# The last row block's sums and stores by two batches, stores from two queues in turn

## Chip, cores and metric

The kernel runs on one core of one Trainium2 chip. The metric is the device time of one execution in microseconds. Each kernel was executed several times; medians are given. Where one execution was profiled, times inside it are counted from the start of its span. The profile page prints a span to 0.1 us; where tails are compared below, they are taken from the unrounded trace.

## The reference

```python
B, S, D = 8, 4224, 192              # batches, tokens, channels
x  = causal 7-tap convolution of x along the tokens, taps = softmax(weight) per head
theta = x @ w_theta                 # 192 x 192
zr, zi = x * cos(theta), x * sin(theta)
y  = w_tok_r @ zr + w_tok_i @ zi    # per batch, 4224 x 4224 token mixing
u  = x + y
out = u + max(u @ w_ch, 0)          # 192 x 192
```

The token mixing is nearly all of the work.

## The kernel before

The 33 row blocks of 128 tokens are finished one after another. For a finished block, `u` (128 x 1536, fp32) lies in the SBUF tile `pv`. It is cast to fp16 (`ub`), transposed (`uT`), multiplied by `wch` into PSUM (`v`), and then, for each half `g` of the eight batches, summed and stored:

```python
def channel_mix(tT, w):
    v = banks("v")                       # one PSUM tile of two banks, two such tiles in turn
    for k in range(2):                   # k: two batches each
        for b in range(2):
            for i in range(2):
                pe(nc.tensor.matmul(v[:, k, b * D : (b + 1) * D], lhsT=tT[:, 3 * k + b + i, :],
                                    rhs=w[:, 2 * b + i, :], start=(i == 0), stop=(i == 1)))
    return v[:, :, 0 : 2 * D]
...
def output(self, i, g):                  # g: four batches, 128 x 768
    u = self.pv[i][:, g * GC : (g + 1) * GC]
    ub = u.rearrange("p (k n) -> p k n", k=2)
    dve(nc.vector.scalar_tensor_tensor(
        out=ub, in0=channel_mix(self.uT[i][:, 6 * g : 6 * g + 6, :], wch), scalar=0.0, in1=ub,
        op0=ALU.max, op1=ALU.add))
    rows = slice(self.tbs[i] * P, (self.tbs[i] + 1) * P)
    nc.sync.dma_start(out=out[g * GB : (g + 1) * GB, rows, :].rearrange("b s d -> s b d"),
                      in_=u.rearrange("p (b d) -> p b d", d=D))
```

`dve` and `pe` keep the order in which the program emits the instructions of an engine. The products of the token mixing (line 443 in the profile) go to other PSUM tiles, named `y`, and their results are added to `pv` by line 408.

Of the kernel before, what the change touches and what calls it, by code (L numbers as in the profile page):

```python
# [10 lines left out]
ALU = mybir.AluOpType  # L11
# [5 lines left out]
def kernel(  # L17
# [23 lines left out]
    nc = tc.nc  # L41
    B, S, D = x.shape
# [13 lines left out]
    GB = 4  # L56
    NG = B // GB
    GC = GB * D
# [8 lines left out]
    NSTEP = start[-1] + NU  # L67
# [10 lines left out]
    def in_order(engine, ins):  # L78
        if engine in last:
            tc.add_manual_dep(ins.ins, last[engine].ins.name, NOSYNC, reason="order")  # L80
        last[engine] = ins
        return ins

    def pe(ins):
        return in_order("pe", ins)

    def dve(ins):
        return in_order("dve", ins)
# [23 lines left out]
    def banks(name, dtype=F32):  # L112
        return mmpool.tile([P, 2, PC if dtype == F32 else 2 * PC], dtype,
                           name=name, tag="mm")
# [9 lines left out]
    wch = constp.tile([P, 4, D], F16, name="wch")  # L124
# [10 lines left out]
    def channel_mix(tT, w):  # L135

        v = banks("v")
        for k in range(2):
            for b in range(2):
                for i in range(2):  # L140
                    pe(nc.tensor.matmul(  # L141
                        v[:, k, b * D : (b + 1) * D], lhsT=tT[:, 3 * k + b + i, :],
                        rhs=w[:, 2 * b + i, :], start=(i == 0), stop=(i == 1),
                    ))
        return v[:, :, 0 : 2 * D]
# [139 lines left out]
    class Step:  # L285
# [185 lines left out]
            crossed(self.uT[i], self.ub[i])  # L471

        def output(self, i, g):
            u = self.pv[i][:, g * GC : (g + 1) * GC]
            ub = u.rearrange("p (k n) -> p k n", k=2)
            dve(nc.vector.scalar_tensor_tensor(  # L476
                out=ub, in0=channel_mix(self.uT[i][:, 6 * g : 6 * g + 6, :], wch), scalar=0.0, in1=ub,
                op0=ALU.max, op1=ALU.add,
            ))
            rows = slice(self.tbs[i] * P, (self.tbs[i] + 1) * P)  # L480
            nc.sync.dma_start(
                out=out[g * GB : (g + 1) * GB, rows, :].rearrange("b s d -> s b d"),
                in_=u.rearrange("p (b d) -> p b d", d=D),
            )

        def outputs(self):

# [75 lines left out]
    for a in range(2):  # L563
        nc.gpsimd.affine_select(
            out=sel, in_=sel, pattern=[[1, Q - 1 + 2 * WR]], channel_multiplier=-1,
# [4 lines left out]
    for a, lo in ((0, True), (1, False)):  # L570
        nc.gpsimd.affine_select(
            out=block[:, a : a + 1], in_=block[:, a : a + 1], pattern=[[0, 1]],
# [7 lines left out]
    def idle(n):  # L580
# [7 lines left out]
        out=wmax, in_=wsb, axis=mybir.AxisListType.X, op=ALU.max  # L588
    ))
    dve(nc.vector.tensor_tensor(  # L590
        out=wsb, in0=wsb, in1=wmax[:, :].unsqueeze(2).to_broadcast([P, H, KS]),
# [6 lines left out]
        out=wsum, in_=wsb, axis=mybir.AxisListType.X, op=ALU.add  # L598
# [5 lines left out]
        out=wdiag, in0=wsb[0:KS, :, :],  # L604
        in1=ident[0:KS, 0:KS].unsqueeze(1).to_broadcast([KS, H, KS]), op=ALU.mult,
# [3 lines left out]
        out=wcol, in_=wdiag, axis=mybir.AxisListType.X, op=ALU.add  # L609
# [5 lines left out]
    for q in range(Q):  # L615
# [7 lines left out]
        out=bands[:, :, 0, :], in0=bv, scalar1=block[:, 0:1]  # L623
    ))
    act(nc.scalar.activation(  # L625
        out=bands[:, :, 1, :], in_=bv, func=AT.Copy, scale=block[:, 1:2]
# [109 lines left out]
```

## Time and profile before

| | |
|---|---|
| three executions, us | 1447.4, 1448.13, 1449.99 (median 1448.13) |
| span of the profiled one | 1446.43 us |
| TensorE busy | 98% of the span |
| end of the last matmul | 1440.85 us |
| from there to the end of the span ("the tail" below) | 5.58 us |

The lines behind this are in the prediction. When a change touches only the end of a program, read the timeline of the end and not the shares of the whole.

### The profile page before, as it was taken

How to read it: one execution, taken by the hardware profiler on the slowest of the kernel's cores; microseconds unless marked ns; L12 is line 12 of the kernel's file. 1: busy time of each engine (PE TensorE's matmuls, PEld its weight loads, DVE VectorE, ACT ScalarE, POOL GpSimd, SP SyncE). 2: the span in 40 equal slices, each digit the busy share in tenths (PEclk: the TensorE clock that was granted, in tenths of full speed). 3: DMA queues.
4: the chain of work that ended last, by engine and by line, in shares of the span. 5: the costliest groups of instructions: out<-in, count | busy, mean ns of one | idle time of the engine just before them, and what ended most of it. 6: DMA issues, size and time to landing. Idle time of an engine off the chain costs nothing.

```text
span 1446.4 us, 23748 instructions
## 1 busy us (share of the span) xinstructions
PE 1416.3 (98%) x9809; PEld 887.9 (61%) x9809; DVE 979.2 (68%) x1051; ACT 315.5 (22%) x379; POOL 435.1 (30%) x655
## 2 busy tenths in 40 slices
PE   7899999999999999999999999999999999999997
PEld 5556666666666666666666666666666666666665
DVE  6893555545548777866666657877777667767686
ACT  5861101111134254000000004435210110010133
POOL 7431211111233232432433342233323123213120
PEclk9999999999999999999999999999999999999999
DMA  9986756465699998998899989999999999998893
GB/s 173 227 178 145 146 103 149 90 149 97 137 231 219 214 250 217 228 254 183 213 256 213 242 143 245 228 188 234 279 216 206 209 204 221 204 203 194 166 222 125
DMA packets 272029, 281.99 MB, mean 195 GB/s; under 512 B 106672, under 2 KB 240176, under 8 KB 271920
## 3 DMA queue, kind: packets, MB, share of 16 engines
q0 software_dynamic: 162464, 92.15, 48.4%
q1 hardware_dynamic: 71824, 178.88, 35.1%
q10 hardware_dynamic: 37632, 9.44, 4.1%
q8 instruction: 77, 1.26, 0.3%
q14 instruction: 32, 0.26, 0.1%
HBM read 245.49 MB, written 108.13 MB: 244 GB/s over the span
## 4 chain that ended last, share of the span: by engine, by line
PE 89%; DVE 4%; DMA 3%; POOL 2%; ACT 1%; issue 1%; SPq 0%; DVEq 0%; ACTq 0%; POOLq 0%
PE y L443 82%; PE v L141 5%; PE pc L210 1%; PE tp L165 1%; POOL st L323 1%; DMA xw<-in_x_dram 1%; DVE z L257 1%; DVE wt L336 1%; DVE pv L408 1%; ACT z L246 1%; DVE z L251 0%; DVE pv L476 0%; DVE wt L348 0%; POOL xw L197 0%; DMA xs<-z 0%
## 5 line engine op out<-in xcount | busy, mean ns | idle before, releaser
L443 PE MATMUL y<-z,wt 128*128 128x384 f16 x7656 | 1283.6, 326 | 10.6 <-DVE pv L408 7.5
L443 PEld LDWEIGHTS <-wt 128*128 128x128 f16 x7656 | 740.8, 98 | 488.6 <-issue 10.6
L408 DVE TENSOR_TENSOR pv<-y,pv 128x768 f32<-128x768 f32 x324 | 308.9, 954 | 323.6 <-PE y L443 282.8
L336 DVE STREAM_TRANSPOSE wt<-st 128x1408 f16<-128x1408 f16 (+7 forms) x224 | 327.8, 1465 | 48.5 <-PE y L443 39.0
L323 POOL DMA_DIRECT2D st<-in_moe_w_tok_r_dram x232 | 132.5, 578 | 466.1 <-DVE wt L336 461.0
L323 POOL DMA_DIRECT2D st<-in_moe_w_tok_i_dram x232 | 132.7, 578 | 404.4 <-DVE wt L336 388.9
L348 DVE TENSOR_TENSOR wt<-wt 128x1408 f16<-128x1408 f16 (+7 forms) x216 | 176.7, 818 | 40.8 <-PE y L443 38.4
L151 ACT ACTIVATE z<-pc 128x768 f16<-128x768 f32 x65 | 53.2, 819 | 387.2 <-PE pc L210 386.9
L151 ACT ACTIVATE ub<-pv 128x768 f16<-128x768 f32 x63 | 50.2, 835 | 333.0 <-DVE pv L408 310.4
L406 ACT ACTIVATE pv<-y 128x768 f32<-128x768 f32 x66 | 54.0, 819 | 282.0 <-PE y L443 282.0
L141 PEld LDWEIGHTS <-uT 128*128 128x128 f16 x1056 | 91.0, 98 | 25.8 <-issue 7.9
L386 POOL TENSOR_TENSOR pv<-pv,xr 128x1536 f32<-128x1536 f32 x24 | 74.5, 3105 | 68.6 <-DVE pv L476 22.1
L197 POOL DMA_DIRECT2D xw<-in_x_dram x132 | 76.4, 585 | 31.0 <-DMA xw<-xw 8.7
L476 DVE SCALAR_TENSOR_TENSOR pv<-v,pv 128x768 f32<-128x768 f32 x66 | 62.9, 954 | 27.5 <-PE v L141 27.1
L257 DVE TENSOR_TENSOR z<-z 128x768 f16<-128x768 f16 x132 | 73.4, 556 | 3.6
L151 ACT ACTIVATE uT<-tp 128x1536 f16<-128x1536 f16 (+1 forms) x48 | 58.2, 1215 | 74.4 <-PE tp L165 74.4
L246 ACT ACTIVATE z<-v,half_pi 128x768 f16<-128x768 f32 x66 | 59.8, 907 | 41.2 <-PE v L141 40.8
L251 DVE TENSOR_TENSOR z<-z 128x1536 f16<-128x1536 f16 x66 | 60.0, 947 | 7.5 <-ACT z L246 7.5
L141 PE MATMUL v<-wth,uT 128*128 128x192 f16 x528 | 55.0, 248 | 4.4 <-ACT z L246 3.0
L141 PE MATMUL v<-wch,uT 128*128 128x192 f16 x528 | 54.2, 246 | 2.1 <-DVE pv L476 1.2
L246 ACT ACTIVATE z<-v 128x768 f16<-128x768 f32 x66 | 53.4, 809 | 0.0
L210 PE MATMUL pc<-xw,bands 96*64 96x192 f16 x528 | 35.8, 258 | 2.6 <-ACT bands L625 1.1
(44 smaller groups left out, 142.4 us busy)
## 6 DMA issues: line engine op xcount, KB each, us to landing
part<-pv SPq DMA_DIRECT2D x79, 768.0 KB, 4.3
pv<-part SPq DMA_DIRECT2D x79, 768.0 KB, 6.1
out_dram<-pv SPq DMA_DIRECT2D x66, 384.0 KB, 4.3
st<-in_moe_w_tok_r_dram POOLq DMA_DIRECT2D x136, 176.0 KB, 5.5
st<-in_moe_w_tok_i_dram POOLq DMA_DIRECT2D x136, 176.0 KB, 5.1
xs<-z SPq DMA_DIRECT2D x132, 96.0 KB, 4.5
xw<-in_x_dram POOLq DMA_DIRECT2D x121, 96.0 KB, 6.1
xr<-xs SPq DMA_DIRECT2D x24, 384.0 KB, 3.7
```

The lines of the kernel that those rows point to most:

```text
L141: pe(nc.tensor.matmul(v[:, k, b * D : (b + 1) * D], lhsT=tT[:, 3 * k + b + i, :], rhs=w[:, 2 * b + i, :], start=(i == 0), stop=(i == 1),))
L151: act(nc.scalar.activation(out=out, in_=in_, func=AT.Copy))
L197: nc.gpsimd.dma_start(out=self.xw[lo : lo + n, h, :, :], in_=x[:, t0 : t0 + n, :].rearrange("b s d -> s b d"),)
L246: act(nc.scalar.activation(**args))
L257: dve(nc.vector.tensor_tensor(out=z[:, o, :], in0=z[:, a, :], in1=z[:, b, :], op=ALU.subtract))
L323: pool(nc.gpsimd.dma_start(out=st[a * Q : (a + 1) * Q, 0:nb, :, 0:n] .rearrange("i r bt s -> i (r bt) s"), in_=w[self.tbs[0] * P : (self.t ...
L336: dve(nc.vector.transpose(self.w[name][:, 0 : self.n, :, :], self.st[int(name[1])][:, int(name[0]) - 1, :, 0 : self.n * Q] .rearrange("p b ...
L348: dve(nc.vector.tensor_tensor(out=self.w[name][:, 0 : self.n, :, :], in0=self.w[a][:, 0 : self.n, :, :], in1=self.w[b][:, 0 : self.n, :, : ...
L386: ins = pool(nc.gpsimd.tensor_tensor(out=self.pv[i], in0=self.pv[i], in1=self.xr[i], op=ALU.add))
L408: dve(nc.vector.tensor_tensor(out=o, in0=yv, in1=o, op=ALU.add))
L443: pe(nc.tensor.matmul(y[cn][:, q, 0:BH], lhsT=self.w[wn][:, c, :, :].rearrange("p bt i -> p (bt i)"), rhs=chunks[k].z[:, zn, q * BH : (q + ...
L476: dve(nc.vector.scalar_tensor_tensor(out=ub, in0=channel_mix(self.uT[i][:, 6 * g : 6 * g + 6, :], wch), scalar=0.0, in1=ub, op0=ALU.max, o ...
```

## The change

The intent: let the last stores start earlier and be shorter. For the last row block only, each sum of four batches becomes two sums of two batches, and each is stored as soon as it is done, by ScalarE's queue and SyncE's in turn.

```diff
-            u = self.pv[i][:, g * GC : (g + 1) * GC]
-            ub = u.rearrange("p (k n) -> p k n", k=2)
-            dve(nc.vector.scalar_tensor_tensor(
-                out=ub, in0=channel_mix(self.uT[i][:, 6 * g : 6 * g + 6, :], wch), scalar=0.0, in1=ub,
-                op0=ALU.max, op1=ALU.add,
-            ))
+            u = self.pv[i][:, g * GC : (g + 1) * GC].rearrange("p (k n) -> p k n", k=2)
+            v = channel_mix(self.uT[i][:, 6 * g : 6 * g + 6, :], wch)
             rows = slice(self.tbs[i] * P, (self.tbs[i] + 1) * P)
-            nc.sync.dma_start(
-                out=out[g * GB : (g + 1) * GB, rows, :].rearrange("b s d -> s b d"),
-                in_=u.rearrange("p (b d) -> p b d", d=D),
-            )
+            ends = self.t == NSTEP - 1
+            for k in (slice(0, 1), slice(1, 2)) if ends else (slice(0, 2),):
+                dve(nc.vector.scalar_tensor_tensor(
+                    out=u[:, k, :], in0=v[:, k, :], scalar=0.0, in1=u[:, k, :],
+                    op0=ALU.max, op1=ALU.add,
+                ))
+                b = slice(g * GB + 2 * k.start, g * GB + 2 * k.stop)
+                dma = nc.scalar.dma_start if ends and k.start == 0 else nc.sync.dma_start
+                dma(
+                    out=out[b, rows, :].rearrange("b s d -> s b d"),
+                    in_=u[:, k, :].rearrange("p k (b d) -> p (k b) d", d=D),
+                )
```

## The prediction

> **What bounds the kernel now.** I read first the summary page: what the whole span is made of, and the size of the groups that the change touches.
>
> ```profile
> span 1446.4 us, 23748 instructions
> PE 1416.3 (98%) x9809; PEld 887.9 (61%) x9809; DVE 979.2 (68%) x1051; ACT 315.5 (22%) x379; POOL 435.1 (30%) x655
> ...
> PE 89%; DVE 4%; DMA 3%; POOL 2%; ACT 1%; issue 1%; SPq 0%; DVEq 0%; ACTq 0%; POOLq 0%
> ...
> L476 DVE SCALAR_TENSOR_TENSOR pv<-v,pv 128x768 f32<-128x768 f32 x66 | 62.9, 954 | 27.5 <-PE v L141 27.1
> ...
> out_dram<-pv SPq DMA_DIRECT2D x66, 384.0 KB, 4.3
> ```
>
> TensorE is busy for 98% of the span and makes 89% of the chain that ended last: this is a matmul-bound kernel. The change touches two of the 66 sums of line 476 and two of the 66 stores, both of the last row block, and no matmul. So only the tail, after the last matmul, can move. Second, the timeline of the last microseconds (start, length, engine, line, operation, count, idle before):
>
> ```profile
> 1438.32 0.96 DVE L476 SCALAR_TENSOR_TENSOR pv<-v,pv 128x768 f32<-128x768 f32 x1 [0.98 <-PE v L141]
> ...
> 1439.33 1.52 PE L141 MATMUL v<-wch,uT 128*128 128x192 f16 x16 [0.21 <-DVE pv L476]
> ...
> 1440.19 1.82 DVE L476 SCALAR_TENSOR_TENSOR pv<-v,pv 128x768 f32<-128x768 f32 x2 [0.91 <-PE v L141]
> ```
>
> TensorE ends at 1439.33 + 1.52 = 1440.85. The first of the two last sums starts at 1440.19, the second follows with no wait, and both are done at 1442.01. The second needs matmuls that were done before it started, so VectorE itself sets this stretch. Third, the store's line, asked for the last two stores alone (issue length in ns, issue start, then microseconds from issue to landing), and, in a second fence, the waits of the SyncE queue (total us, times, longest):
>
> ```profile
> L481 SPq DMA_DIRECT2D out_dram<-pv x1: 372/372/372, 1441.2 to 1441.2; - x1
> ...
> DMA to landing us min/median/max: 2.5/2.5/2.5
> ...
> L481 SPq DMA_DIRECT2D out_dram<-pv x1: 372/372/372, 1442.0 to 1442.0; - x1
> ...
> DMA to landing us min/median/max: 2.7/2.7/2.7
> ```
>
> ```profile
> SPq L731 <- DMA out_dram<-pv: 2.2, 1, 2.2
> ```
>
> After the last store is issued, the program only waits for it: 2.2 us on SyncE, then the closing steps. The store lands at 1442.0 + 2.7 = 1444.7, and the span ends at 1446.4, so 1.7 us of closing follow. Fourth, busy shares by stretch; in each line the last two numbers are the DMA share and GB/s, and the one before them TensorE's granted clock:
>
> ```profile
> 1441.40:1441.50 0.10, 0.00 (x0) 0.00 (x0) 0.10 (x1) 0.00 (x0) 0.00 (x0) 1.00 0.01 0
> ...
> 1442.00:1442.10 0.10, 0.00 (x0) 0.00 (x0) 0.01 (x1) 0.00 (x0) 0.00 (x0) 1.00 0.09 31
> 1442.10:1442.20 0.10, 0.00 (x0) 0.00 (x0) 0.00 (x0) 0.00 (x0) 0.00 (x0) 1.00 0.73 253
> ...
> 1443.10:1443.20 0.10, 0.00 (x0) 0.00 (x0) 0.00 (x0) 0.00 (x0) 0.00 (x0) 1.00 1.09 354
> ...
> 1444.20:1444.30 0.10, 0.00 (x0) 0.00 (x0) 0.00 (x0) 0.00 (x0) 0.00 (x0) 1.00 0.47 139
> ```
>
> The DMA engines are empty from 1441.4 to 1442.1, then full without a gap to about 1444.3. Both last stores run back to back through them: 2 x 393,216 bytes in 2.2 us, about 360 GB/s. This is the real limit of the tail. The last store does not wait for its own issue; it waits behind the one before it (2.7 us to landing where the undisturbed one has 2.5). Hence the end is: first data of the second-last store, plus 2.2 us of transfer, plus 0.4 us to landing (1444.3 to 1444.7), plus 1.7 us of closing. Only the start of that busy stretch is open to the change.
>
> **What the Trainium skill says.** "DMA: Bandwidth & Descriptors", section "Issuing engines are not separate DMA queues", says that transfers started from several engines share the same 16 DMA engines, and that a second issuing engine saves only the issue time. The trace agrees as far as it goes: two adjacent stores run at one store's rate (369 and 376 GB/s in neighbouring stretches), but both came from one queue. "Perfetto Trace Analysis", section "DMA Optimizations", says that splitting a DMA may let a part start sooner where the DMA engines are idle. That is the idle stretch from 1441.4 to 1442.1 here. The same page, section "DMA Instruction — HWDGE (DVE, Sync)", shows a descriptor generator shared by the issuing sequencers, with a lock wait inside the profiled issue time. This trace has 372 ns for most stores, but 712 ns for the one issued at 1437.4, 1.0 us after another, which might be such a wait. "VectorE: DVE Perf Modes", section "Why PSUM operands drop a tier", allows fp32 with a PSUM operand one element per cycle; at that page's 0.96 GHz, 768 columns take 800 ns. The measured 954 ns leaves about 154 ns fixed. Back to back the second sum started before the first had ended: 1.82 - 0.96 = 0.86 us from start to start, so only about 0.06 us of the fixed part shows.
>
> **The change part by part.** I compared the instruction order of both kernels, apart from line numbers. TensorE and GpSimd are the same, instruction by instruction. VectorE has four sums of 128x384 in place of two of 128x768; the second and fourth have no wait of their own. SyncE keeps two stores, halved, and ScalarE gets two at its end, where it is idle (the timeline has its last work at 1439.15 for 0.81 us). Nothing earlier changes. Each first half waits for all eight matmuls of its result, since its partner has no wait of its own; so no sum starts earlier than 1440.19.
>
> - Sums: half a sum is estimated as 400 + 154 = 554 ns, and 400 + 60 = 460 ns from start to start. Starts 1440.19, 1440.65, 1441.11, 1441.57; ends about 1440.74, 1441.20, 1441.66, 1442.12. Two more instructions cost 2 x 0.06 = 0.12 us at the end, but the first part is ready at 1440.74, not at 1441.15: 0.41 us earlier.
> - Issues: 0.03 to 0.05 us after each end, at about 1440.78, 1441.24, 1441.70 and 1442.16. In before, first data came 0.9 us after the issue started (1441.2 to 1442.1). I take this for all four, from either queue.
> - Transfers: first data could come at 1441.68, 1442.14, 1442.60 and 1443.06. The store ahead of them has left the engines by 1441.4, so the first starts at once. Each needs 2.2/4 = 0.55 us, more than the 0.46 us between them, so the engines are full from 1441.68 until 1441.68 + 2.2 = 1443.88. The last quarter could start at 1443.06 and finish at 1443.61 by itself, so the queue of bytes, and not the later last sum, still sets the end.
> - Sum: 1444.3 - 1443.9 = 0.4 us earlier; landing and closing move along. The 0.12 us on VectorE stay beside the transfers and cost nothing.
>
> The total is 1448.13 - 0.4 = 1447.7 us, 0.03% less.
>
> **The rivals.**
> First: the halves are worth more. If the end were set by the last store alone, without a queue ahead of it, halving it would save 0.55 us and the later sum would return 0.12: also 0.43 us. It would show as empty DMA stretches between the quarters. The gapless stretch speaks against it, and the time would hardly tell.
> Second: issue costs take the gain back. Four issues 0.46 us apart share a generator; if each took 0.7 us, as the one store of 712 ns did, issues from 1440.78 on would run to about 1443.6, first data of the last would come 0.55 us after that (the gap from an issue's end to its data in before: 1441.57 to 1442.1), and its end at 1444.7: 0.4 us slower, 1448.5. For it speaks the one 712; against it, the pair 0.86 us apart with 372 each.
> Third: nothing is visible. A ScalarE issue may have a longer way to first data, and its two halves may land late through one slow engine (two stores of the tail took 3.1 us, not 2.5). Then the gain is 0 to 0.2 us, 1448.0.
> None of them reaches 2%, which is 29 us: from the last sum's start to the end of the span there are only 6 us.
>
> **Range and chances.** The effect is between -0.5 and +0.4 us. Three runs of before span 1447.4 to 1449.99, so the spread of runs is larger than the effect. I take 1446.3 to 1449.3. A 2% change would need something that the instruction order excludes, or a slow execution: faster 0.003, same 0.992, slower 0.005.
>
> **What would show the steps right or wrong.** In the changed kernel's profile: four sums of 128x384 of about 554 ns, the last ending near 1442.1 of a comparable span; DMA busy from about 1441.7, gapless for 2.2 us; the last landing 0.4 us earlier measured from the last matmul's end (3.85 us after it in before, about 3.45 then). Wrong would be: issues much over 372 ns, a gap between the quarters, ScalarE's data more than 0.9 us after its issue, or a sum longer than 600 ns. The total itself can fail by the spread of runs alone.

## The result, and the profile after

| | before | changed |
|---|---|---|
| executions, us | 1447.4, 1448.13, 1449.57, 1449.99 | 1447.82, 1449.12, 1450.23, 1452.22 |
| median | 1448.85 | 1449.67 |
| span of the profiled one | 1446.43 | 1446.11 |
| tail | 5.58 | 5.29 |

The ratio is 1.0007 with a 95% interval from 0.9989 to 1.0026: no difference is seen. (A ratio is the mean time of one kernel's fast executions over that of the other's in the same rounds, so not quite the ratio of the medians.) "Within 2%" is as foreseen, but the median of 1449.67 lies above the stated range, which ended at 1449.3. And yet the profiled execution is shorter than that of before, and its tail is too.

The timeline of the changed kernel's end (columns as in the prediction):

```profile
1439.30 1.52 PE L141 MATMUL v<-wch,uT 128*128 128x192 f16 x16 [0.22 <-DVE pv L480]
...
1440.16 1.95 DVE L480 SCALAR_TENSOR_TENSOR pv<-v,pv 128x384 f32<-128x384 f32 x4 [0.91 <-PE v L141]
1440.75 1.31 ACTq L486 DMA_DIRECT2D out_dram<-pv  x2
```

The last matmul ends at 1439.30 + 1.52 = 1440.82, against 1440.85 before: nothing ahead of the tail has moved in this pair of profiles. The four half sums run from 1440.16 to 1442.11 (estimated: 1442.12), and the first half store is issued at 1440.75 (estimated: 1440.78), where the first store of before was issued at 1441.2.

The first and the last of the four stores (issue time, start, and time to landing), then the shares by stretch at the two ends of their transfer (the last two numbers are the DMA share and GB/s):

```profile
L486 ACTq DMA_DIRECT2D out_dram<-pv x1: 397/397/397, 1440.8 to 1440.8; - x1
DMA to landing us min/median/max: 2.0/2.0/2.0
...
L486 SPq DMA_DIRECT2D out_dram<-pv x1: 372/372/372, 1442.1 to 1442.1; - x1
DMA to landing us min/median/max: 2.4/2.4/2.4
```

```profile
1441.60:1441.70 0.10, 0.00 (x0) 0.00 (x0) 0.10 (x2) 0.00 (x0) 0.00 (x0) 1.00 0.13 46
1441.70:1441.80 0.10, 0.00 (x0) 0.00 (x0) 0.10 (x1) 0.00 (x0) 0.00 (x0) 1.00 0.89 307
...
1443.80:1443.90 0.10, 0.00 (x0) 0.00 (x0) 0.00 (x0) 0.00 (x0) 0.00 (x0) 1.00 0.94 259
1443.90:1444.00 0.10, 0.00 (x0) 0.00 (x0) 0.00 (x0) 0.00 (x0) 0.00 (x0) 1.00 0.04 8
```

The engines fill at 1441.7 and empty at 1443.9. The estimate was 1441.68 to 1443.88. Measured from the last matmul's end, the last data are through after 3.14 us, where it was 3.50 before: 0.36 us earlier. The last store lands after 3.69 us, where it was 3.85: only 0.16 us earlier, because its landing came 0.55 us after the last data and not 0.34. What follows the landing then took 1.60 us and not 1.73, so 0.29 us reach the end of the span (5.58 - 5.29). Up to the last data the mechanism is the predicted one, and the change gains about 0.3 us. The landing did not move along as predicted. The question is why the total is outside the range.

One more line of this profile will be needed below. In the view of the DMA queues from 1442.0 to 1444.4, an instruction fetch (kind "instruction") lies among the last stores; it started 3.05 us after the last matmul's end. In the kernel before there is none in that stretch.

```profile
q14 instruction: 1, 0.01, 1.4%
```

### The profile page after: what moved, and what is told of

Its sections match the earlier page's. It is cut to its first block, busy times and chain, and to the rows that moved or that the text cites. A ratio compares the mean times of both kernels' runs of the same rounds, so it can differ in the third digit from the quotient of the medians.

```text
span 1446.1 us, 23755 instructions
## 1 busy us (share of the span) xinstructions
PE 1415.9 (98%) x9809; PEld 887.7 (61%) x9809; DVE 979.4 (68%) x1053; ACT 315.4 (22%) x379; POOL 434.9 (30%) x655
## 4 chain that ended last, share of the span: by engine, by line
PE 89%; DVE 3%; DMA 3%; ACT 2%; POOL 1%; issue 1%; SPq 0%; DVEq 0%; ACTq 0%; POOLq 0%
PE y L443 82%; PE v L141 5%; PE pc L210 1%; PE tp L165 1%; DMA xw<-in_x_dram 1%; DMA xw<-xw 1%; POOL st L323 1%; ACT z L246 1%; DVE pv L408 1%; DVE z L257 1%; DVE z L251 1%; DMA pv<-part 1%; DVE wt L336 1%; DVE pv L480 0%; DMA st<-in_moe_w_tok_r_dram 0%
## 5 line engine op out<-in xcount | busy, mean ns | idle before, releaser
L480 DVE SCALAR_TENSOR_TENSOR pv<-v,pv 128x768 f32<-128x768 f32 (+1 forms) x68 | 63.1, 931 | 27.5 <-PE v L141 27.0
```

## The experiments

Every kernel below gave correct results. Runs r1 to r8 were on one chip, r9 to r11 on a second, r12 and r13 on a third; ratios are always against the kernel before on the same chip. Profiles of r5, r6 and r9 to r11 come from single executions, of which I use only the traces, not the times. The theory to test: the change moves only the tail, and the miss is scatter between executions. The rival: the change costs about 1 us somewhere ahead of the tail.

### r1: the changed kernel again

No edit.

> The changed kernel, run again with more rounds, to tell an effect from spread. Measure 1: the tail, from the end of the last matmul to the end of the span in the profile; it was 5.58 us before (1446.43 - 1440.85) and 5.29 us after (1446.11 - 1440.82). Measure 2: the ratio of the times to those of the kernel before. Theory (the change moves only the tail, by -0.3 us, and the miss of the range is spread between executions): tail 5.2 to 5.4 us, start of the last matmuls of the kernel unchanged within the spread, ratio 0.999 to 1.001 with an interval that holds 1. Rival (the change costs about 1 us somewhere ahead of the tail, which would explain 1449.67): ratio 1.0005 or more again, with the interval above 1, and the last matmul ending 1 us later than before in the profile.

Measured: median 1449.23 us (1448.13 to 1450.48), ratio 0.9999 (0.9986 to 1.0013), tail 5.28 us. The last matmul ended 0.43 us later than in the profile of before, and all of that had arisen in the first 48 us, long before any changed instruction. The rival's extra microsecond is not there.

### r2: the kernel before against itself

No edit to the kernel before.

> The kernel before against itself: a control without any change. Theory of spread: the ratio is off 1 by up to 0.001 either way, single runs lie from about 1447.4 to 1452 us, and the tail is 5.5 to 5.7 us. Rival (executions of one program agree to a few tenths of a us, and the 1.5 us between the two medians were the change): all runs within 1 us, ratio within 0.0002 of 1.

Measured: median 1450.39 us, single executions from 1448.14 to 1457.82 us, ratio 1.0013 (0.9992 to 1.0034), tail 5.60 us. An unchanged kernel differs from itself by as much as the changed one does. The tail, on the other hand, repeats to 0.02 us. This falsifies the rival's picture that executions agree to some tenths.

### r3 and r9: the split, all four stores from SyncE

```diff
-                dma = nc.scalar.dma_start if ends and k.start == 0 else nc.sync.dma_start
+                dma = nc.sync.dma_start
```

> Sums and stores split as in the change, but all four half stores issued by SyncE. Theory (the earlier start of the first half is the gain; an issue of 0.37 us fits between halves 0.46 us apart, so the second queue is not needed): tail 5.2 to 5.4 us as with the change, DMA busy without a gap over the four halves, issues of about 0.37 us each. Rival (the second queue is what gains): the fourth half is held up by the issues ahead of it, and the tail is 5.5 us or more.

> The split with all four half stores from SyncE, once more, since its tail of 5.42 us lay between the two theories: most engines had finished the data 3.3 us after the last matmul's start, as with the change, but one engine carried data for 0.6 us more, after an instruction fetch on the DMA engines that fell into the stores. Theory (one queue is as good as two, and the fetch held up one engine): without a fetch inside the four stores the tail is 5.25 to 5.35 us; with one it is 5.4 or more again and one engine is late again. Rival (one queue is worse by itself): 5.4 us or more with no late engine.

Measured: tails of 5.46 and 5.68 us, and in r3 the ratio 1.0005 (0.9989 to 1.0020). The issues took 0.37 to 0.45 us, and the last began 1.46 and 1.47 us after the last matmul's end, where it was 1.32 with the change. In both runs the bulk of the data was through some 3.0 us after the last matmul's end, as with the change, but a small flow went on for over half a microsecond, as on one late engine. The first fence shows a stretch of r3, by its busy shares, 3.2 to 3.4 us after the last matmul's end; the second is from the view of the DMA queues of r9, cut to its last stores (queue and kind, then packets, MB, share):

```profile
1446.50:1446.70 0.20, 0.00 (x0) 0.00 (x0) 0.00 (x0) 0.00 (x0) 0.00 (x0) 1.00 0.07 23
```

```profile
q1 hardware_dynamic: 465, 0.33, 52.8%
q14 instruction: 2, 0.02, 3.5%
```

A share of 0.07 is about one engine of 16. Two instruction fetches (queue 14) fell among the stores; in the same view of the kernel before, from 1442.0 to 1444.4, there is none. So "one queue is as good as two" did not come true: both times it was worse than the change, and r9's 5.68 us is no better than the 5.58 of before. A fetch lay among the stores and an engine was late both times. But the changed kernel also has a fetch among its stores, in all three of its profiles, 3.05 to 3.06 us after the last matmul's end, and there the data do not trail; in r3 and r9 the first fetch came at 2.5 us. Whether an earlier fetch holds up an engine stays open, since no run moved the fetch alone. With the sums split, a second queue thus cannot be called needless.

### r4: whole sums and stores, the first of the last two from ScalarE

```diff
-            nc.sync.dma_start(
+            dma = nc.scalar.dma_start if self.t == NSTEP - 1 and g == 0 else nc.sync.dma_start
+            dma(
                 out=out[g * GB : (g + 1) * GB, rows, :].rearrange("b s d -> s b d"),
```

> Sums and stores whole as before; only the first of the last two stores goes by the ScalarE queue. Theory (the tail is set by when the first data can start, and by the bytes): tail 5.5 to 5.65 us, as before. Rival (the second queue lets the two stores overlap or lands them sooner): tail 5.4 us or less, and DMA rates over 380 GB/s while both run.

Measured: tail 5.68 us, just above the stated range, ratio 1.0005 (0.9989 to 1.0020), DMA rates as before. ScalarE's issue took 0.41 us, not 0.37, and its data came 0.04 us later; the last store landed 0.03 us later, and the rest of the 0.1 us arose after the landing. In this one profile a second queue by itself gains nothing.

### r5 and r10: the sums split, the stores whole

```diff
-                b = slice(...); dma = ...; dma(out=out[b, rows, :]..., in_=u[:, k, :]...)   # inside the loop
+            nc.sync.dma_start(out=out[g * GB : (g + 1) * GB, rows, :]..., in_=u...)          # after the loop
```

> The sums split in two, the stores whole and from SyncE as before. Measured in the profile, from the last matmul's end to the span's end (5.55 us before, 5.28 and 5.32 with the change). Theory (only the earlier first data gains; the split itself costs VectorE 0.06 us per added sum): the sums end 1.28 us after the last matmul, not 1.16, and the tail is 5.55 to 5.7 us, no gain. Rival (shorter sums alone gain): tail 5.4 us or less.

> The split sums with whole stores, once more, since its tail of 5.94 us was 0.25 us above the range stated. Theory (0.1 us of it is the later sums, the rest a late landing of that execution): 5.55 to 5.75 us. Rival (split sums with whole stores are worse by 0.3 us or more by themselves): 5.9 us or more again, with the last store landing 2.9 us after its issue.

Measured: tails of 5.97 us both times. No gain, as the theory has it, but 0.4 us worse than before and not 0.1: here the stated range failed twice, and in r10 the sign that the rival had named came true (5.9 us or more, and 2.9 us to landing). The sums ended 1.29 us after the last matmul (1.16 before), as estimated; the rest lies in the last store, which took 2.9 us to land in both runs (2.7 before). An instruction fetch started within 0.01 us of the end of the last data in both. Why it cost 0.27 us is not settled. Over all 15 profiles there is a pattern: the last landing came 0.34 to 0.35 us after the last data in the five without a fetch near the end of the data (before, r2, r4, r6, r12), and 0.52 to 0.64 us after it in the ten with one. But these ten are also the kernels with split sums, so no run tells the fetch from the split.

### r6: the sums whole, the stores split over two queues

```diff
+            dve(nc.vector.scalar_tensor_tensor(out=u, in0=v, scalar=0.0, in1=u, op0=ALU.max, op1=ALU.add))
             for k in (slice(0, 1), slice(1, 2)) if ends else (slice(0, 2),):
-                dve(nc.vector.scalar_tensor_tensor(out=u[:, k, :], in0=v[:, k, :], ...))
```

> The sums whole, each stored in two halves on the two queues. Theory: no half can start before the whole sum is done, the four halves carry the same bytes, so the tail is 5.5 to 5.7 us, no gain. Rival (halved stores on two queues move faster or land sooner by themselves): tail 5.4 us or less.

Measured: tail 5.53 us. Smaller stores by themselves give 0.05 us, all of it after the last landing (3.85 us after the last matmul, as before). Each pair of issues began together, and they took 0.37 us on SyncE and 0.47 us on ScalarE, so most of an issue does not wait for the other queue. With r4, r5 and r10 this shows that no part of the change gains by itself. It needs a half sum, and a half store that leaves as soon as that is done; what r3 and r9 leave open is the share of the second queue.

### r7 and r11: a PSUM tile for each half of the last block

The halves of the first four batches go to the `y` tiles, which are free by then, those of the last four to the usual ones:

```diff
+    def half_mix(tT, w, k, own):
+        v = ypool.tile([P, 2, PC], F32, name="y", tag="y") if own else banks("v")
+        return channel_mix(tT, w, (k,), v)            # only the four matmuls of half k
...
-            v = channel_mix(self.uT[i][:, 6 * g : 6 * g + 6, :], wch)
+            halves = [half_mix(t, wch, k, g == 0) for k in range(2)] if ends else None
```

> The change, and each half of the last row block's channel mix in a PSUM tile of its own, the first pair in the tiles that the big products have left free. Then a half sum waits for four matmuls, not eight, and the first mix no longer waits for the sum ahead of it (a wait of 0.2 us that ended at 1439.3 in the kernel before). The last matmul moves, so the measure is from the last matmul of line 443 to the span's end: 15.0 us before and in its control, 14.75 and 14.8 with the change. Theory (the end is the first data plus the bytes at about 360 GB/s, and the store ahead of these four then sets the start): sums start 0.5 to 0.9 us earlier, DMA busy without a gap from the store ahead on, 14.3 to 14.5 us. Rival (something else, such as the last sum or the landing, sets the end): 14.7 us or more. In the median of the times none of it will show: executions of one program differ by 1 to 6 us.

> The version with PSUM tiles of its own, once more. Measured from the start of the last transposes to the end of the span: 7.8 us before, 7.5 with the change, 7.1 in the first run of this version. Theory: 7.05 to 7.2 us. Rival (the first run was luck): 7.4 us or more.

The end of r11, to be set beside the fences of before and after:

```profile
1437.62 0.51 PE L170 MATMUL tp<-ident,ub 128*128 128x128 f16 x6 [0.40 <-ACT ub L156]
1437.97 0.82 PE L141 MATMUL y<-wch,uT 128*128 128x192 f16 x8
1439.04 0.83 PE L141 MATMUL v<-wch,uT 128*128 128x192 f16 x8 [0.24 <-ACT uT L156]
```

The first mix now follows the transposes without a wait. From the start of those transposes to the end of the span it is 7.11 us in r7 and 1444.73 - 1437.62 = 7.11 in r11, against 7.82 before and 7.53 with the change. This is 0.42 us better than the change and 0.71 us better than before. The DMA engines were full without a gap from the store ahead of these four to the last data, so bytes are the limit from there on. The median of r7 shows little of it, as expected: 1448.98 us, ratio 0.9994 (0.9979 to 1.0010). (I had named the end of line 443's last matmul as the mark; by it r7 has 14.33 us, inside the stated 14.3 to 14.5, where before has 15.05. The transposes are the equivalent mark that the timeline shows for all kernels.)

### r8: the changed kernel a third time, for the scatter

> The changed kernel a third time, for the spread. In the profiles so far an execution has one stretch of 3.4 us in which TensorE's granted clock is 0.50, about 39 us from the start, and the one that was 2.4 us longer had a second. Theory (the spread between executions of one program is the number of such stretches, each worth up to 1.7 us, and a few tenths of a us in the first 48 us): times scatter over 1446 to 1453 us again, executions with a mean clock of 0.998 are shorter by 1 us or more than those of 0.995 to 0.997, and in the profile all difference to the other profiles arises either in the first 48 us or at a stretch of halved clock. Rival (the spread comes from DMA traffic all along): the difference grows gradually over the span, and the clock tells nothing of the time.

Measured: median 1449.77 us (1446.73 to 1452.35), ratio 1.0002 (0.9987 to 1.0017), tail 5.28 us. To see where executions differ, I compared the start of every matmul of each profile with that of before. The differences do not grow gradually. They arise in the first 48 us (up to 1 us either way), and in r3, r7 and r8 by a step of 1.67 us between 100 and 110 us. What remains are a few smaller steps (0.3 and 0.6 us in r7, one of 0.35 us in r5, 0.2 us or less elsewhere) with flat stretches between them; these come without a halved clock, which the expectation did not allow for. Here is that step by stretches, in the kernel before (no step), in r3 and in r8 (the number ahead of the last two is the granted clock):

```profile
99.00:105.00 6.00, 3.54 (x23) 1.93 (x22) 5.76 (x9) 0.00 (x0) 0.97 (x2) 1.00 0.61 88
105.00:110.00 5.00, 5.00 (x33) 2.99 (x32) 5.00 (x6) 0.63 (x1) 2.44 (x5) 1.00 0.70 85
```

```profile
105.00:110.00 5.00, 4.64 (x19) 2.32 (x20) 3.56 (x5) 0.00 (x0) 3.17 (x6) 0.66 0.48 57
```

```profile
99.00:105.00 6.00, 3.54 (x21) 1.89 (x19) 5.79 (x8) 0.00 (x0) 1.07 (x2) 0.94 0.52 72
105.00:110.00 5.00, 5.00 (x25) 2.64 (x24) 3.56 (x5) 0.00 (x0) 2.33 (x4) 0.73 0.77 100
```

In r3 the mean clock of these 5 us is 0.66, which is 3.4 us at half clock: 5 x (1 - 0.66)/0.5. TensorE is "busy" for nearly all of them, but does 19 matmuls where it did 33. A busy share alone would hide this. And just ahead of it TensorE is idle for 6.00 - 3.54 = 2.46 us, in every profile up to r11; this is the timeline of r8:

```profile
104.08 8.19 PE L443 MATMUL y<-z,wt 128*128 128x384 f16 x39 [2.46 <-DVE pv L408]
```

The Trainium skill, "TensorE: Matmul & The Clock Gate", section "Part 1: The HAM clock gate (the "warmup" mystery)", says that TensorE runs at half rate after an idle window of about 3.4 us, and that the windows are free-running, not started with the kernel. The traces agree with the free-running grid: in r3 the two halved stretches start 68.27 us apart, 20 times 3.413 us. Laying that grid over the idle gap of 13 profiles (r1 to r11, before and after) splits them cleanly. In the three with the step, one window holds 2.6 us of idle time, the whole gap (measured from matmul start to matmul start, less 0.16 us). In all three the halved stretch begins where that window ends (105.92 us in r3). In the ten without, a boundary cuts the gap, and no window holds more than 1.8 us of it. The starting phase of an execution thus seems to decide whether it loses 1.67 us.

The mean clock of an execution goes with its time, though the two groups overlap, and an execution of r8 with a clock of 1.000 took 1449.99 us. Over the 70 executions with a recorded clock, of all kernels but r12 and r13:

| mean clock | executions | median us | from, to |
|---|---|---|---|
| 0.998 to 1.000 | 31 | 1447.9 | 1445.94, 1451.25 |
| 0.994 to 0.997 | 39 | 1450.1 | 1448.75, 1457.82 |

The mean clock cannot say which stretch was halved. The gap at 105 us is not the only place: most profiles hold another halved stretch at about 38 us, as the expectation of r8 says. Here it is in the kernel before and, missing, in r12 (below):

```profile
38.00:43.00 5.00, 4.55 (x30) 2.98 (x31) 4.83 (x8) 2.65 (x5) 2.63 (x5) 0.66 0.89 131
```

```profile
38.00:43.00 5.00, 3.88 (x40) 2.93 (x41) 4.91 (x8) 3.45 (x6) 2.55 (x5) 1.00 0.71 97
```

It is missing in r5, r9, r11 and r13 too; r5, r9 and r11 were 0.5 to 1.0 us ahead of the kernel before by 48 us. Among the 13 profiles, the three with the step are just the three with a mean clock of 0.997 or less. But of the other 57 executions 36 have such a clock, so the profiles hold too few of the slow kind to say what slowed those.

### r12 and r13: filling the idle gap

To test the gap as the cause, 14 matmuls of no use go into it. They read constants and write a PSUM tile that nobody reads:

```diff
             for r, (wn, zn, cn, opens, to) in enumerate(runs):
+                if self.t == 3 and r == 5:
+                    warm = banks("warm")
+                    for _ in range(14):
+                        pe(nc.tensor.matmul(warm[:, 0, 0 : 2 * D], lhsT=ident, rhs=wth[:, 0:2, :],
+                                            start=True, stop=True))
```

r12 is the kernel before with this, r13 the kernel of r7 with it.

> The kernel before, with 14 matmuls of no use placed into TensorE's one idle stretch of 2.46 us at 102 us (they read constants, write a free PSUM tile that nobody reads, and end before the wait does). Theory (the spread between executions is mainly one stretch of halved clock at about 105 us, which comes in those executions where a fixed 3.4 us window of the clock control happens to hold most of that idle gap; it costs 1.67 us): in no profile a halved clock at 105 us, few or no executions with a mean clock of 0.995 to 0.997, and the median 0.5 to 1.7 us below that of the kernel before in the same rounds, with a smaller scatter. Rival (the halved clock comes by chance, or from power, and not from the gap): half of the executions again at 0.997 or less, the median within 0.4 us of the kernel before.

> The change, the PSUM tiles of its own for the last row block, and the idle stretch at 102 us filled. Theory: the sum of both, 0.7 us from the tail (7.1 us from the start of the last transposes to the end of the span, where it was 7.8) and 0.5 to 1.7 us in the median from the clock; median 1.2 to 2.4 us below the kernel before in the same rounds, most executions from 1446 to 1448 us. Rival (the clock is not moved by the gap): 0.7 us or less below, half of the executions over 1449 us.

The timeline of r12 at the former gap, and its clock:

```profile
101.17 2.44 PE L439 MATMUL warm<-wth,ident 128*128 128x384 f16 x14
103.78 8.46 PE L450 MATMUL y<-z,wt 128*128 128x384 f16 x51 [0.18 <-DVE pv L408]
```

```profile
105.00:110.00 5.00, 5.00 (x33) 2.99 (x32) 5.00 (x6) 0.81 (x1) 2.33 (x4) 1.00 0.79 87
```

The fillers take 2.44 us and leave 0.18 us of waiting: the real matmuls start when they would have. The full clock in the one profile each of r12 and r13 says little by itself, as ten of the 13 unfilled profiles had it too. Measured on this chip, in the same rounds: the kernel before 1449.45 us (1445.94 to 1451.66, 11 executions); r12 1448.21 us (1447.33 to 1454.07, 6); r13 1447.26 us (1446.34 to 1448.03, 5). Ratios: r12 0.9998 (0.9982 to 1.0013), r13 0.9987 (0.9975 to 1.0000). Of the kernel before, 5 of 11 executions had a mean clock of 0.997 or less; of the two filled kernels, 2 of 11. Ten of the 11 filled executions took 1448.53 us or less, and 6 of the 11 unfilled ones took over 1449.4.

This agrees with the gap as one cause of the scatter, but does not show it: by chance alone a split at least as uneven as 2 and 5 of 11 would come in about a third of such comparisons (Fisher's exact test), and r13 owes part of its lower times to its shorter tail. That the halved stretch follows where the gap lies in the grid is shown by 13 profiles, with a limit that was drawn after they were seen. How much of the scatter it makes is open. Two expectations were not met in full: in r12 two executions had a clock of 0.996 and 0.997, and one of them took 1454.07 us, which keeps r12's mean where it was. Other slow stretches exist, then; no profile has caught one of the executions over 1451 us, and their cause stays open. r13 is the best version found, 0.13% ahead of the kernel before, with an interval that just touches 1; its tail (7.10 us by the mark of r7) repeats.

## Why the prediction was right or wrong

- Bound and place of the change: right. TensorE and everything ahead of the tail are as before; r1 shows differences only in the first 48 us, where no instruction was changed.
- Sums: right. Ends of 1442.12 against 1442.11, with 0.12 us added on VectorE that cost nothing here.
- Issues: right within 0.03 us, but ScalarE's first took 0.40 us and not 0.37. The second rival (issues of 0.7 us) did not occur with the change.
- Transfers: right. Full from 1441.7 to 1443.9, gapless. ScalarE's first data came 0.92 us after its issue, SyncE's in before 0.91. r5 and r6 agree that an earlier first half is needed; r4 shows that a second queue alone gains nothing, but r3 and r9 that without it the gain shrinks (5.46 us) or is gone (5.68).
- Landing and closing "move along": wrong. The last landing was to come about 3.45 us after the last matmul's end and came after 3.69 (3.85 before), 0.2 us later after the last data than in before. The closing was 0.13 us shorter. So 0.36 us of earlier data became 0.29 us of earlier end, the same within 0.01 us in r1 and r8. The third rival had a late landing, but of ScalarE's halves: these landed in 1.98 and 2.12 us, and SyncE's last one in 2.37. This is small against the miss.
- The step that failed is the range: "Three runs of before span 1447.4 to 1449.99, so the spread of runs is larger than the effect. I take 1446.3 to 1449.3." The spread was named and then not used. Its upper end was set below one of the three times in hand. And three executions were taken for the centre: 1448.13 was near the fast kind. Over all 34 executions of the kernel before, the control included, the median is 1449.47 us and they reach from 1445.94 to 1457.82; over 16 of the changed one it is 1449.67, from 1446.73 to 1452.35, and 9 of those 16 lie above 1449.3. With the effect exactly right, the range would still have failed more often than not.
- What stands in its place: a scatter of 11.9 us between executions of the unchanged kernel (1445.94 to 1457.82). Grouped by mean clock, there are two kinds, about 2 us apart and nearly equally frequent. One contribution is measured: the halved clock after one idle gap of TensorE, 1.67 us in three of 13 profiles. The rest of the cause is open. The profile of before had this gap in view (2.46 us idle, released by line 408) and its times probably held both kinds. The one profiled was of the short kind, so its trace did not show the step.

## What to carry to other kernels

Judge a change to a program's tail by the tail in the trace, from the last event that it cannot touch: 0.29 us repeated to 0.02 us there, while whole times scattered by 6 us and more. Before setting a range, look for kinds of execution in the times and mean clocks that you have, and set the range over the kinds. An idle gap of the matmul engine may cost more than its length, by the clock that follows; filling it with matmuls of no use took no time here, and slow clocks were rarer with it (2 of 11 executions, against 5 of 11), too few to be sure. And at an end bound by stores, start the first bytes earlier; a queue added without that gained nothing.

## What the Trainium skill lacked or had wrong

- "TensorE: Matmul & The Clock Gate", section "Why this matters for your kernels", warns of idle gaps of more than about 3 us. Here a gap of 2.46 us was enough, in each of the three profiles where one window of the 3.413 us grid held all of it; with at most 1.8 us of it in one window, none of ten profiles lost the clock. The page has the grid, and the starting phase for the warm-up, but not that a shorter gap in mid-kernel seems to make the time of an execution a matter of its phase (1.67 us a time).
- "DMA: Bandwidth & Descriptors", section "Issuing engines are not separate DMA queues", says that a second issuing engine only saves issue time. r4 agrees for whole stores, and adds a cost: the issue took 0.41 us from ScalarE and 0.37 us from SyncE, and the tail of that one profile was 0.1 us longer.
- "Runtime: NRT & Kernel Launch", section "Instruction fetch mechanics", has instruction fetches by DMA, but no page that I found tells that they may fall among a kernel's last stores. In both runs of the one-queue split two fetches did, the data of what looks like one DMA engine trailed by over half a microsecond, and the tail was 5.46 and 5.68 us in place of 5.28 to 5.29. With a fetch near the end of the data the last landing came 0.52 to 0.64 us after it, without one 0.34 to 0.35; that the fetch is the cause is not shown.
